# Three quarters of an expert's first product by Strassen's seven products, with operands reloaded from DRAM and sums kept in SBUF

## The chip, the core and the metric

The kernel runs on one core of one Trainium2 chip. The core has TensorE for matrix products (it writes to PSUM), VectorE (DVE in the profile), ScalarE (ACT), GpSimd (POOL) and SyncE (SP), which issues the transfers here. The metric is the device time of one launch in microseconds (us), the median of the timed runs.

## The reference

Attention without a softmax, and two experts one after the other, on 4608 tokens (8 batches of 576) with 512 features:

```python
kv = einsum('bhsd,bhse->bhde', k, v)           # per batch and head, 64 x 64
out = einsum('bhsd,bhde->bhse', q, kv)
x = out / sqrt(mean(out * out) + 1e-6) * g_norm    # then [4608, 512]

h = x @ w_in                                   # first expert: 512 -> 2048
x = (h * cos(h)) @ w_out                       # 2048 -> 512

h = x @ w_in2                                  # second expert: 512 -> 1024
s = h * softmax(h)
x = (s - mean(s)) / sqrt(var(s) + 1e-6) * g_ln @ w_out2   # 1024 -> 512
```

All inputs and the output are 32-bit floats (the weights come as 64-bit words and are converted on the chip).

## The kernel before

Each large product is made three times, for accuracy: every operand is split into a high part (a rounded copy, written by ScalarE) and a low part (the rest, a subtraction on VectorE or GpSimd), and the helper `mm3` adds high x high, high x low and low x high into one PSUM bank. Its three lines are L175, L176 and L177. A matmul takes 128 x 128 weights and up to 512 columns.

**First expert.** The hidden units are cut into four quarters, one pass over all tokens for each. A pass has 9 blocks of 512 tokens and 4 chunks of 128 hidden units, so 36 steps. `step_h` makes the chunk's hidden values: 4 x 3 matmuls into one of two banks, then ScalarE and VectorE in turn (scale to an integer, L590; difference, L592; sine, L595; product, L598; high part, L600; low part, L601). `step_out` adds the chunk's part of the output to four banks (`acc0` to `acc3`), 4 x 3 matmuls, one step later. After four chunks `evac` takes the four banks: in pass 1 it copies them, in passes 2 to 4 it adds the sum so far, loaded from DRAM (`px2`, L618), on VectorE (L628), and stores it again (L633). So each of the four passes has 36 x 24 matmuls. x stays in SBUF for all passes and is split again for each (`prep_x`: ScalarE L562, GpSimd L567). The weights of the next pass are converted and split during a pass (`convert`, four VectorE operations L502 to L509; `split_w`).

**Pass 1** also holds the attention, in small matmuls between the steps (L372, L431, and transposes L462).

**Second expert.** Two token tiles of 128 form a pair, 18 pairs. The first product is already made by Strassen's scheme: the pair's rows and the features are cut into halves, four sums on GpSimd (L660) give the operands (`prep_pair`), and seven products of 2 x 3 matmuls replace eight (`second`). Seven sums on VectorE (L698) put the result together; each product starts a new one of four banks. Then follow the softmax and the norm (`soft`), 16 transposes (L771) and two times 24 matmuls (`second_out`).

**Order.** Everything is handed to a planner (`Flow`), which orders the work of each engine once, before the launch, from a duration and a due time per task. Each engine runs its queue in that order and waits on semaphores. SyncE's queue, which issues the transfers, is one of them. The planner never runs a task of GpSimd beside one of VectorE that has no operand in PSUM (`port`).

## Time and profile before

| | |
|---|---|
| median of 3 timed runs | 1299.99 us (1299.46 to 1300.11) |
| span of the profiled execution | 1297.6 us (2.4 us below that median) |
| busy: TensorE, VectorE, ScalarE, GpSimd | 98%, 68%, 53%, 35% |
| TensorE's granted clock, whole span | 0.996 |
| transfers | 139.58 MB, 108 GB/s |

The span runs from the first to the last instruction of the profiled execution, 1297.6 us; its own time has no other reading here, and the timed runs are other executions. Busy is the time in which an engine had an instruction in work. PEld is the loading of weights, which runs beside TensorE's matmuls. A row of a view names the line, the engine, the operation, and what it writes `<-` what it reads.

### The profile page before, as it was taken

Reading aid. Unit: us, or ns where it says so; the run is one execution under the profiler, and the core shown is the slowest. Engines: PE = TensorE matmul, PEld = TensorE weight load, DVE = VectorE, ACT = ScalarE, POOL = GpSimd, SP = SyncE. Lnnn points to the kernel's source line nnn. Section 1 sums busy time; section 2 is a strip of 40 time slices with the busy share of each in tenths; the row PEclk is TensorE's granted clock in tenths of the full one; section 3 lists DMA queues with packets and bytes.
Section 4 is the critical chain, followed back from the end, with each engine's and each line's share of the span. In section 5 each row is a group of like instructions: output and inputs, shape, how many; then the busy total and the mean of one; then the engine's idle time right before and its main releaser. Section 6 shows DMA issues by size and latency. Waiting matters only on the chain.

```text
span 1297.6 us, 17765 instructions
## 1 busy us (share of the span) xinstructions
PE 1276.8 (98%) x6468; PEld 1056.6 (81%) x6468; DVE 884.1 (68%) x1421; ACT 681.3 (53%) x1211; POOL 460.3 (35%) x437
## 2 busy tenths in 40 slices
PE   5999999999999999999999999999999999999998
PEld 4788888888888888888888888887888888888886
DVE  6885444688965457645454868788978787777854
ACT  4676455666554445454545555546454445444532
POOL 2336354557551337231313465432242222221100
PEclk8999999999999999999999999999999999999999
DMA  9654442243543244323233444544110111010000
GB/s 320 219 175 134 142 142 88 77 136 119 176 127 117 78 127 133 109 86 108 88 100 112 142 134 143 187 150 138 52 63 17 65 50 62 21 57 25 25 25 33
DMA packets 62407, 139.58 MB, mean 108 GB/s; under 512 B 7408, under 2 KB 10480, under 8 KB 61168
## 3 DMA queue, kind: packets, MB, share of 16 engines
q1 hardware_dynamic: 62320, 138.45, 33.2%
q8 instruction: 51, 0.84, 0.3%
q14 instruction: 36, 0.29, 0.1%
HBM read 91.23 MB, written 47.19 MB: 107 GB/s over the span
## 4 chain that ended last, share of the span: by engine, by line
PE 95%; DMA 1%; DVE 1%; ACT 1%; POOL 1%; issue 0%; SPq 0%; DVEq 0%; ACTq 0%
PE ps_acc L175 15%; PE ps_acc L177 15%; PE ps_acc L176 15%; PE ps_h L175 14%; PE ps_h L177 14%; PE ps_h L176 14%; PE ps_o L431 2%; PE ps_acc L771 2%; PE ps_o L372 1%; PE ps_o L462 1%; DMA att<-qkv 1%; DMA xt<-qkv 1%; POOL att L446 1%; DVE xt L738 0%; ACT xt L468 0%
## 5 line engine op out<-in xcount | busy, mean ns | idle before, releaser
L567 POOL TENSOR_TENSOR xhl<-xt,xhl 128x512 fp32r<-128x512 f32 (+3 forms) x176 | 191.9, 1120 | 227.6 <-ACT xhl L562 227.5
L175 PE MATMUL ps_acc<-temps,wpool 128*128 128x512 f32 x648 | 255.1, 394 | 0.0
L177 PE MATMUL ps_acc<-temps,wpool 128*128 128x512 f32 x648 | 252.5, 390 | 0.0
L176 PE MATMUL ps_acc<-temps,wpool 128*128 128x512 f32 x648 | 252.3, 389 | 0.0
L175 PE MATMUL ps_h<-xhl,wpool 128*128 128x512 f32 x576 | 228.0, 396 | 0.2 <-DVE temps L598 0.2
L177 PE MATMUL ps_h<-xhl,wpool 128*128 128x512 f32 x576 | 224.7, 390 | 0.0
L176 PE MATMUL ps_h<-xhl,wpool 128*128 128x512 f32 x576 | 224.6, 390 | 0.0
L592 DVE SCALAR_TENSOR_TENSOR temps<-ps_h,temps 128x512 f32<-128x512 f32 x144 | 99.2, 689 | 132.4 <-ACT temps L590 132.3
L601 DVE TENSOR_TENSOR temps<-temps,temps 128x512 fp32r<-128x512 f32 x144 | 124.5, 865 | 66.6 <-ACT temps L600 64.5
L590 ACT ACTIVATE temps<-ps_h 128x512 int32<-128x512 f32 x144 | 86.1, 598 | 142.2 <-PE ps_h L177 141.2
L595 ACT ACTIVATE temps<-temps,const 128x512 f32<-128x512 f32 x144 | 104.2, 724 | 89.7 <-DVE temps L592 89.5
L177 PEld LDWEIGHTS ps_acc<-temps,wpool 128*128 128x128 f32 x648 | 121.6, 188 | 25.9 <-DVE wpool L525 0.5
L175 PEld LDWEIGHTS ps_acc<-temps,wpool 128*128 128x128 f32 x648 | 121.7, 188 | 25.2 <-issue 0.3
L176 PEld LDWEIGHTS ps_acc<-temps,wpool 128*128 128x128 f32 x648 | 121.8, 188 | 24.2
L598 DVE TENSOR_TENSOR temps<-ps_h,temps 128x512 f32<-128x512 f32 x144 | 98.9, 687 | 59.6 <-ACT temps L595 59.4
L600 ACT CAST temps<-temps 128x512 fp32r<-128x512 f32 x144 | 89.4, 621 | 90.2 <-DVE temps L598 84.8
L175 PEld LDWEIGHTS ps_h<-xhl,wpool 128*128 128x128 f32 x576 | 108.4, 188 | 23.1 <-DVE temps L598 0.6
L177 PEld LDWEIGHTS ps_h<-xhl,wpool 128*128 128x128 f32 x576 | 108.4, 188 | 22.9
L176 PEld LDWEIGHTS ps_h<-xhl,wpool 128*128 128x128 f32 x576 | 108.5, 188 | 21.5
L562 ACT CAST xhl<-xt 128x512 fp32r<-128x512 f32 (+3 forms) x192 | 90.3, 510 | 10.0 <-PE ps_h L177 8.9
L754 POOL TENSOR_TENSOR xt<-xt,const 128x1 f32<-128x1 f32 x36 | 23.0, 639 | 196.1 <-DVE xt L751 188.6
L777 DVE TENSOR_TENSOR wpool<-ps_acc,wpool 128x512 fp32r<-128x512 f32 x72 | 46.6, 685 | 42.7 <-ACT wpool L774 42.7
(130 smaller groups left out, 2236.4 us busy)
## 6 DMA issues: line engine op xcount, KB each, us to landing
px<-temps SPq DMA_DIRECT2D x144, 256.0 KB, 2.7
temps<-px SPq DMA_DIRECT2D x108, 256.0 KB, 3.8
xt<-w SPq DMA_DIRECT2D x27, 512.0 KB, 4.6
att<-qkv SPq DMA_DIRECT2D x24, 512.0 KB, 5.1
rawp<-w SPq DMA_DIRECT2D x21, 512.0 KB, 3.9
xt<-px SPq DMA_DIRECT2D x9, 1024.0 KB, 5.3
out<-temps SPq DMA_DIRECT2D x36, 256.0 KB, 2.0
att<-qkv SPq DMA_DIRECT2D x24, 288.0 KB, 5.6
```

Of the source, the lines that this page charges most:

```text
L175: PE.matmul(ps, lhsT=lh, rhs=rh, start=start, stop=False)
L176: PE.matmul(ps, lhsT=lh, rhs=rl, start=False, stop=False)
L177: PE.matmul(ps, lhsT=ll, rhs=rh, start=False, stop=stop)
L562: ACT.copy(out=buf["xh", i][:, k, a - m * TB:a - m * TB + n], in_=xt(k, a, n))
L567: eng.tensor_tensor(out=buf["xl", i][:, k, r], in0=xt(k, a, n), in1=f(buf["xh", i][:, k, r]), op=ALU.subtract)
L590: add("ACT", 0.61, lambda: ACT.activation(out=buf["kk"], in_=h(), func=AF.Copy, scale=INV_2PI, bias=0.25), r=[hb], w=["kk"], at=at)
L592: add("DVE", 0.71, lambda: DVE.scalar_tensor_tensor(out=buf[tk], in0=h(), scalar=INV_2PI, in1=buf["kk"], op0=ALU.mult, op1=ALU.subtract), ...
L595: add("ACT", 0.74, lambda: ACT.activation(out=buf[tk], in_=buf[tk], func=AF.Sin, bias=buf["halfpi"][:, 0:1], scale=2 * math.pi), r=[tk, "h ...
L598: add("DVE", 0.71, lambda: DVE.tensor_tensor(out=buf[tk], in0=h(), in1=buf[tk], op=ALU.mult), r=[hb, tk], w=[tk], at=at, ps=True)
L600: add("ACT", 0.64, lambda: ACT.copy(out=buf[ghk], in_=buf[tk]), r=[tk], w=[ghk], at=at + 2)
L601: add("DVE", 0.71, lambda: DVE.tensor_tensor(out=buf[glk], in0=buf[tk], in1=f(buf[ghk]), op=ALU.subtract), r=[tk, ghk], w=[glk], at=at + 2)
L777: DVE.tensor_tensor(out=buf["ll", n][:, part, :], in0=tr(), in1=f(buf["lh", n][:, part, :]), op=ALU.subtract)
```

## The change

Pass 1 stays. The other three quarters of the first expert become 15 **items**: a block of token tiles by one quarter. The blocks hold 3, 3, 4, 4 and 4 pairs of tiles (`BLOCKS`), so a matmul has 384 columns in the first two and 512 in the others (one column per token of one half of the pairs). A quarter has two halves of 256 hidden units. `first_h` makes one half for the block by seven products; the tokens' two halves, the features' two halves and the hidden units' two halves are the 2 x 2 quarters of Strassen's scheme. Three of the products are added in PSUM to a bank that holds an earlier one (`more=True`), the other sums are VectorE's. `first_out` makes the output part as before and adds it to sums in SBUF (`acc`), which are loaded before a block's first quarter and stored after its last.

x no longer stays in SBUF: pass 1 writes it to DRAM (`xd`), and each block loads it, forms the sums on GpSimd, and splits them (`prep`, L624 and L391/L392), once for its three quarters. The weights of these quarters, and those of the second expert, are converted and split once, during pass 1 and the items, and written to DRAM (`wid`, `wod`, `bd`, `lwd`); each item loads its own into two buffers (`reload_in`, `reload_out`). The low parts of the items' activations are GpSimd's (L674). The second expert's products use the same scheme with adding in PSUM, so five sums on VectorE (L859).

```diff
-NPASS, CPP = 4, 4
+BLOCKS = (0, 3), (6, 3), (12, 4), (20, 4), (28, 4)
...
-    def evac(ps_, m, px, at):
...
-                add("DVE", 0.71, lambda d=d, sk=sk: DVE.tensor_tensor(out=buf[sk], in0=buf[ACC[d]][:, 0:TB], in1=buf[sk],
-                                                                      op=ALU.add), r=[ACC[d], sk], w=[sk], at=at, ps=True)
...
+    def reload_in(fp, at):
+        s = fp % 2
+        for n_, (pos, n) in enumerate(((B11, 2), (T1, 2), (T3, 2), (T4, 1))):
+            wide = slice(pos * 256, (pos + n) * 256)
+            add("SP", 0.8 * n, lambda wide=wide: SP.dma_start(out=f(rwi(s)[:, :, wide]), in_=wid[fp, :, :, wide]),
+                r=[("wid", fp, o) for o in range(pos, pos + n)], w=[("wi", s, o) for o in range(pos, pos + n)],
+                at=at + 2 * n_, lat=2.0)
...
+    def first_h(T, s, at, step):
...
+        def prod(bk, a, b, t, more=False):
+            for kk in range(2):
+                def mm(kk=kk):
+                    w = slice(b * 256 + kk * P, b * 256 + kk * P + P)
+                    x = rx(a)
+                    mm3(buf[bk][:, 0:n], rwi(s)[:, 0, w], rwi(s)[:, 1, w], x[:, 0, kk, 0:n], x[:, 1, kk, 0:n],
+                        kk == 0 and not more, kk == 1, more)
...
+        prod(bA, A11, B11, at)
...
+        prod(bB, S2, T2, at + d)
+        plus(v1, bB, v0, at + 2 * d + E_)
+        prod(bC, S1, T1, at + 2 * d)
+        plus(v2, bC, v1, at + 3 * d + E_)
+        prod(bA, A12, B21, at + 3 * d, more=True)
+        chain(bA, True, 0, 0, at + 4 * d)
+        prod(bB, S3, T3, at + 4 * d)
+        plus(v2, bB, v2, at + 5 * d + E_)
+        chain(v2, False, 1, 1, at + 5 * d)
+        prod(bC, S4, B22, at + 5 * d, more=True)
+        plus(bC, bC, v1, at + 6 * d + E_)
+        chain(bC, True, 1, 0, at + 6 * d)
+        prod(bB, A22, T4, at + 6 * d, more=True)
+        plus(bB, bB, v1, at + 7 * d + E_)
+        chain(bB, True, 0, 1, at + 7 * d)
...
+    def first_out(item, half, at, step):
...
+            if item["first"]:
+                add("SP", e_(0.8, 0.4, n), lambda ak=ak, place=place: SP.dma_start(out=parted(buf[ak][:, 0:n], T), in_=place()),
+                    r=pk, w=[ak], at=t - 16, lat=2.0)
+            for c in range(4):
...
+                    mm3(buf[bk][:, 0:n], w[:, 0, :], w[:, 1, :], rg(m)[:, 0, 0:n], rg(m)[:, 1, 0:n], c == 0, c == 3)
...
+            add("DVE", e_(0.71, 0.44, n), lambda ak=ak, bk=bk: DVE.tensor_tensor(
+                out=buf[ak][:, 0:n], in0=buf[bk][:, 0:n], in1=buf[ak][:, 0:n], op=ALU.add),
+                r=[bk, ak], w=[ak], at=t - 4, ps=True)
```

`rx` are the split operands of x (single, written anew for each block), `rwi` and `rwo` the two buffers for weights, `rg` twelve places for activations. A `chain` is the cosine with its two parts.

Three places of the order. First TensorE in the middle of the first expert. Before, where in pass 4 a chunk's hidden values end and an output part begins (`ps_acc` are the output's banks, `ps_h` those of the hidden values):

```order
L177 MATMUL ps_h_142<-xhl_91,wpool_70 128x512
L175 MATMUL ps_h_142<-xhl_91,wpool_70 128x512
L176 MATMUL ps_h_142<-xhl_91,wpool_70 128x512
L177 MATMUL ps_h_142<-xhl_91,wpool_70 128x512
L175 MATMUL ps_h_142<-xhl_91,wpool_70 128x512
L176 MATMUL ps_h_142<-xhl_91,wpool_70 128x512
L177 MATMUL ps_h_142<-xhl_91,wpool_70 128x512
L175 MATMUL ps_acc_129<-temps_96,wpool_70 128x512 [waits Activation_49]
L176 MATMUL ps_acc_129<-temps_96,wpool_70 128x512 [waits DVE_49]
L177 MATMUL ps_acc_129<-temps_96,wpool_70 128x512
L175 MATMUL ps_acc_130<-temps_96,wpool_70 128x512
L176 MATMUL ps_acc_130<-temps_96,wpool_70 128x512
```

After the change, in the first item, the last product of one half and one of the other half (`ps_167` and `ps_163` are banks, `rxb`, `rxa` the operands of x, `rwi_794` and `rwi_795` the two buffers for weights):

```order
L171 MATMUL ps_0_167<-rxb_2474,rwi_794 128x384 [waits DVE_49]
L172 MATMUL ps_0_167<-rxb_2474,rwi_794 128x384
L173 MATMUL ps_0_167<-rxb_2474,rwi_794 128x384
L171 MATMUL ps_0_167<-rxb_2474,rwi_794 128x384
L172 MATMUL ps_0_167<-rxb_2474,rwi_794 128x384
L173 MATMUL ps_0_167<-rxb_2474,rwi_794 128x384
L171 MATMUL ps_0_163<-rxa_81,rwi_795 128x384
L172 MATMUL ps_0_163<-rxa_81,rwi_795 128x384
L173 MATMUL ps_0_163<-rxa_81,rwi_795 128x384
L171 MATMUL ps_0_163<-rxa_81,rwi_795 128x384
L172 MATMUL ps_0_163<-rxa_81,rwi_795 128x384
L173 MATMUL ps_0_163<-rxa_81,rwi_795 128x384
```

Where four times three matmuls of 512 columns stood for a chunk, each product has two times three, here of 384 columns; the first waits for VectorE.

Second TensorE in the last products of a pair of the second expert. Before, three products in three banks (`late_r` and `wpool` hold the weights' parts, `xhl_91` the pair's):

```order
L175 MATMUL ps_h_1_6711<-wpool_69,xhl_91 128x512
L176 MATMUL ps_h_1_6711<-wpool_69,xhl_91 128x512
L177 MATMUL ps_h_1_6711<-wpool_69,xhl_91 128x512
L175 MATMUL ps_h_0_2167<-late_r_4276,xhl_91 128x512 [waits DVE_49]
L176 MATMUL ps_h_0_2167<-late_r_4277,xhl_91 128x512
L177 MATMUL ps_h_0_2167<-late_r_4276,xhl_91 128x512
L175 MATMUL ps_h_0_2167<-wpool_69,xhl_91 128x512
L176 MATMUL ps_h_0_2167<-wpool_69,xhl_91 128x512
L177 MATMUL ps_h_0_2167<-wpool_69,xhl_91 128x512
L175 MATMUL ps_h_1_2168<-late_r_4278,xhl_91 128x512 [waits DVE_49]
L176 MATMUL ps_h_1_2168<-late_r_4279,xhl_91 128x512
L177 MATMUL ps_h_1_2168<-late_r_4278,xhl_91 128x512
```

After, the end of the product S3 T3, the product S4 B22, and the start of A22 T4:

```order
L171 MATMUL ps_0_187<-rxa_81,rwi_795 128x512
L172 MATMUL ps_0_187<-rxa_81,rwi_795 128x512
L173 MATMUL ps_0_187<-rxa_81,rwi_795 128x512
L171 MATMUL ps_0_191<-rxa_81,rwi_795 128x512 [waits DVE_49]
L172 MATMUL ps_0_191<-rxa_81,rwi_795 128x512
L173 MATMUL ps_0_191<-rxa_81,rwi_795 128x512
L171 MATMUL ps_0_191<-rxa_81,rwi_795 128x512
L172 MATMUL ps_0_191<-rxa_81,rwi_795 128x512
L173 MATMUL ps_0_191<-rxa_81,rwi_795 128x512
L171 MATMUL ps_0_187<-rxb_2474,rwi_795 128x512 [waits DVE_49]
L172 MATMUL ps_0_187<-rxb_2474,rwi_795 128x512
L173 MATMUL ps_0_187<-rxb_2474,rwi_795 128x512
```

The product A22 T4 now goes to the bank of S3 T3, `ps_187`, with one product between; the wait for VectorE at its start is for the sum that reads this bank.

Third VectorE. Before, where pass 2 ends and pass 3 begins (`temps` are the cosine's and the running sum's buffers, `rawp` a weight chunk in conversion):

```order
L592 SCALAR_TENSOR_TENSOR temps_95<-ps_h_142,temps_95 128x512 [waits Activation_49]
L628 TENSOR_TENSOR temps_97<-ps_acc_129,temps_97 128x512 [waits DMAHW6_49,PE_49]
L628 TENSOR_TENSOR temps_98<-ps_acc_130,temps_98 128x512 [waits DMAHW7_49,PE_49]
L598 TENSOR_TENSOR temps_95<-ps_h_142,temps_95 128x512 [waits Activation_49]
L628 TENSOR_TENSOR temps_99<-ps_acc_131,temps_99 128x512 [waits DMAHW0_49,PE_49]
L628 TENSOR_TENSOR temps_100<-ps_acc_132,temps_100 128x512 [waits DMAHW3_49,PE_49]
L601 TENSOR_TENSOR temps_96<-temps_95,temps_96 128x512 [waits Activation_49]
L502 TENSOR_SCALAR rawp_2174<-rawp_2174 128x512 [waits Activation_49]
L592 SCALAR_TENSOR_TENSOR temps_95<-ps_h_141,temps_95 128x512 [waits Activation_49]
L504 SCALAR_TENSOR_TENSOR rawp_2174<-rawp_2172,rawp_2174 128x512 [waits DMAHW4_49,DVE_49]
L509 SCALAR_TENSOR_TENSOR rawp_2177<-rawp_2173,rawp_2177 128x512
L598 TENSOR_TENSOR temps_95<-ps_h_141,temps_95 128x512 [waits Activation_49]
```

After, at the first item of tokens 2560 to 3583 (`mid` and `fh` hold the output sums, `rxa` and `rxb` the new operands of x, `fconv` a weight chunk in conversion):

```order
L805 TENSOR_TENSOR mid_2483<-ps_0_183,mid_2483 128x512 [waits PE_49]
L805 TENSOR_TENSOR fh_115<-ps_0_171,fh_115 128x512 [waits PE_49]
L392 TENSOR_TENSOR rxb_2474<-xf_110,rxb_2474 128x4x128 [waits DMAHW5_49,Activation_49]
L392 TENSOR_TENSOR rxb_2474<-xf_110,rxb_2474 128x2x128 [waits Activation_49]
L365 TENSOR_SCALAR fconv_101<-fconv_101 128x512
L805 TENSOR_TENSOR fh_115<-ps_0_175,fh_115 128x512 [waits PE_49]
L367 SCALAR_TENSOR_TENSOR fconv_101<-fconv_101 128x512 [waits DMAHW2_49,DVE_49]
L392 TENSOR_TENSOR rxb_2474<-xf_111,rxb_2474 128x4x128 [waits DMAHW7_49,Activation_49]
L392 TENSOR_TENSOR rxa_80<-sf_105,rxa_80 128x4x128 [waits Activation_49]
L392 TENSOR_TENSOR rxb_2474<-xf_111,rxb_2474 128x2x128 [waits Activation_49]
L805 TENSOR_TENSOR mid_2478<-ps_0_179,mid_2478 128x512 [waits PE_49]
L370 TENSOR_SCALAR fconv_101<-fconv_101 128x512 [waits DVE_49]
```

Between the output sums (L805) now stand the splits of the block's x (L392) and the conversions (L365, L367), in one queue.

## Rows read from the trace of the kernel before

**Rows 1.** Head of the page: span; busy us, share, instructions of each engine.

```profile
span 1297.6 us, 17765 instructions
...
PE 1276.8 (98%) x6468; PEld 1056.6 (81%) x6468; DVE 884.1 (68%) x1421; ACT 681.3 (53%) x1211; POOL 460.3 (35%) x437
```

**Rows 2.** The page's chain that ended last, by engine and by line.

```profile
PE 95%; DMA 1%; DVE 1%; ACT 1%; POOL 1%; issue 0%; SPq 0%; DVEq 0%; ACTq 0%
PE ps_acc L175 15%; PE ps_acc L177 15%; PE ps_acc L176 15%; PE ps_h L175 14%; PE ps_h L177 14%; PE ps_h L176 14%; PE ps_o L431 2%; PE ps_acc L771 2%; PE ps_o L372 1%; PE ps_o L462 1%; DMA att<-qkv 1%; DMA xt<-qkv 1%; POOL att L446 1%; DVE xt L738 0%; ACT xt L468 0%
```

**Rows 3.** Stages by time: length, busy us of each engine, granted clock, DMA.

```profile
core 0: us, PE busy (x) PEld busy (x) DVE busy (x) ACT busy (x) POOL busy (x), PEclk, DMA share, GB/s
30.00:294.00 264.00, 262.86 (x1780) 217.33 (x1777) 166.04 (x254) 166.24 (x311) 123.21 (x114) 1.00 0.44 141
294.00:886.00 592.00, 591.83 (x2611) 489.58 (x2610) 387.13 (x569) 306.52 (x538) 243.92 (x210) 1.00 0.40 125
887.00:1297.60 410.60, 405.13 (x1917) 335.09 (x1915) 311.64 (x564) 195.24 (x342) 84.09 (x100) 1.00 0.12 45
```

**Rows 4.** Timeline of TensorE in pass 3: start, length drawn, line.

```profile
599.62 0.39 PE L175 MATMUL ps_h<-xhl,wpool 128*128 128x512 f32 x1
...
605.06 0.39 PE L175 MATMUL ps_h<-xhl,wpool 128*128 128x512 f32 x1
```

**Rows 5.** Weight loads by line and form: busy us, mean ns.

```profile
L175 PEld LDWEIGHTS ps_h<-xhl,wpool 128*128 128x128 f32 x576 | 108.4, 188 | 23.1 <-DVE temps L598 0.6 <-issue 0.3
```

**Rows 6.** Timeline of TensorE in the second expert: transposes, next matmul.

```profile
1011.41 1.04 PE L771 MATMUL ps_acc<-const,xt 128*128 128x128 f32 x8
1012.20 0.49 PE L175 MATMUL ps_h<-late_r,xhl 128*128 128x512 f32 x1
```

**Rows 7.** Views of single lines: ns min/median/max, first and last start.

```profile
L601 DVE TENSOR_TENSOR temps<-temps,temps x144: 674/692/1795, 43.5 to 886.5; 128x512 fp32r<-128x512 f32 x144
...
L598 DVE TENSOR_TENSOR temps<-ps_h,temps x144: 673/691/693, 40.6 to 885.0; 128x512 f32<-128x512 f32 x144
...
L678 DVE TENSOR_TENSOR xhl<-xt,xhl x72: 409/681/1220, 860.2 to 1228.7; 128x512 fp32r<-128x512 f32 x54, 128x256 fp32r<-128x256 f32 x18
...
L502 DVE TENSOR_SCALAR rawp<-rawp x21: 413/419/1511, 251.8 to 520.0; 128x512 uint32<-128x512 uint32 x21
...
L504 DVE SCALAR_TENSOR_TENSOR rawp<-rawp,rawp x21: 675/686/1791, 254.2 to 525.8; 128x512 uint32<-128x512 uint32 x21
...
L676 ACT CAST xhl<-xt x72: 389/623/651, 859.4 to 1224.9; 128x512 fp32r<-128x512 f32 x54, 128x256 fp32r<-128x256 f32 x18
...
L567 POOL TENSOR_TENSOR xhl<-xt,xhl x176: 450/1280/1812, 108.5 to 840.0; 128x512 fp32r<-128x512 f32 x88, 128x256 fp32r<-128x256 f32 x32, 128x384 fp32r<-128x384 f32 x28, 128x128 fp32r<-128x128 f32 x28
...
L525 POOL TENSOR_TENSOR wpool<-rawp,wpool x21: 1285/1299/1752, 259.2 to 535.9; 128x512 fp32r<-128x512 f32 x21
...
L660 POOL TENSOR_TENSOR xt<-xt x36: 726/736/1747, 846.3 to 1207.1; 128x256 f32<-128x256 f32 x36
```

**Rows 8.** The cosines' first VectorE operation in pass 1 (0 to 294 us).

```profile
L592 DVE SCALAR_TENSOR_TENSOR temps<-ps_h,temps x36: 676/691/694, 37.3 to 293.8; 128x512 f32<-128x512 f32 x36
```

**Rows 9.** L601 in the page's costliest groups: busy us, mean ns.

```profile
L601 DVE TENSOR_TENSOR temps<-temps,temps 128x512 fp32r<-128x512 f32 x144 | 124.5, 865 | 66.6 <-ACT temps L600 64.5
```

**Rows 10.** The first 100 us by time (columns as in rows 3).

```profile
0.00:25.00 25.00, 12.79 (x124) 11.06 (x124) 13.82 (x28) 8.88 (x16) 8.61 (x14) 0.93 0.96 325
25.00:100.00 75.00, 72.24 (x585) 59.74 (x585) 63.77 (x112) 51.70 (x98) 27.08 (x28) 0.95 0.61 200
```

**Rows 11.** DMA issues of the page: count, KB each, us to landing.

```profile
temps<-px SPq DMA_DIRECT2D x108, 256.0 KB, 3.8
```

**Rows 12.** Timeline of TensorE at the start of the second expert.

```profile
907.68 0.50 PE L177 MATMUL ps_acc<-wpool,wpool 128*128 128x512 f32 x1 [0.91 <-DVE wpool L777]
```

**Rows 13.** Timeline: last matmul of a product, then its sum.

```profile
1016.43 0.39 PE L177 MATMUL ps_h<-late_r,xhl 128*128 128x512 f32 x1
...
1016.85 0.68 DVE L698 TENSOR_TENSOR xt<-ps_h,temps 128x512 f32<-128x512 f32 x1
```

More of the change, by code (lines that the diff above doesn't have):

```diff
@@ new lines, in open_e2, with parted, rwi, rwo @@
+    def open_e2():
+        close_pool("rg2")
+        open_pool("e2a", side="right")
+    BANKS = [("bank", i) for i in range(8)]
+    for i in range(8):
+        declare(f"ps{i}", ("bank", i), 0, [P, 512])
+        open_pool(f"ps{i}", space=PSUM)
+    def parted(ap, l=2):
+        return ap.rearrange("p (l n) -> p l n", l=l)
+    def rwi(s):
+        return parted(buf["rwi", s])
+    def rwo(s):
+        return buf["rwo", s].rearrange("p (d j l n) -> p d j l n", d=KC, j=2, l=2)
+    def rg(m):
+        return parted(buf["rg", m])
@@ new lines, in tile_kernel, with att_bank @@
+    stage = Ring(("st", i) for i in range(7))
+    hvs = Ring(("hv", i) for i in range(4))
+    tts = Ring(("tt", i) for i in range(3))
+    xfs = Ring(("xf", i) for i in range(2))
+    xns = Ring(("xn", i) for i in range(2))
+    sfs = Ring(("sf", i) for i in range(2))
+    wss = Ring(range(2))
+    early = [*BANKS[2:8]]
+    late_att = Ring(BANKS[6:8])
+    accs = Ring(BANKS[2:6])
+    hbank = Ring([BANKS[0], BANKS[1], BANKS[6], BANKS[7]])
+    def att_bank():
+        return early.pop(0) if early else late_att()
@@ L408, in parts @@
         return res
+    held = {}
     def tile_slots(g):
-        bks = [next_bank() for _ in range(2)]
+        bks = [att_bank() for _ in range(2)]
         def heads(ap):
@@ new lines, in tile_kernel, with end_step @@
+    n_jobs = len(jobs)
+    last = None
+    closed = False
+    def end_step(m, c, j, at):
+        step_out(c, j, at)
+        if c == CPP - 1:
+            block_out(m, at)
+    for i in range(NSTEP):
+        m, c = divmod(i, CPP)
+        at, d = t_step(i), STEP_A
+        if c == 0 and m + 1 < NB:
+            run_slots(needs[m + 1] - pos, at + SLOT_LATE, SLOT_RATE, needs[m + 1])
+        if pos == len(slots) and not closed and m == NB - 2:
+            closed = True
+            flow.change(open_p1, ("att",), ("rx0", "rx1", "rx6", "mid", "rg2x"))
+            flow.change(lambda: None, ("p0s",), ("p1h",))
+            for g in range(NU - 2, NU):
+                pair_prep(g, at)
+            stage.keys, stage.n = [("st", i) for i in range(4, 7)], 0
+        while jobs and (n_jobs - len(jobs)) * (JOB1 - JOB0) <= (i - JOB0) * n_jobs:
+            jobs.pop(0)(at + JOB_AT)
+        step_h(m, c, i % 2, at)
@@ L914, in tile_kernel @@
         if last:
             end_step(*last)
-        if ps_ and c == 1:
-            px = load_px(m, at - 4)
-        last = (ps_, m, c, i % 2, px, at + 2.5 * d)
-        block = ps_ * NB + m + 1
-        if c == 1 and block < NPASS * NB:
-            prep_x(block, at + 2)
-            if ps_ == NPASS - 1:
-                for part in range(NX):
-                    if m * TB < (part + 1) * XP - TB <= (m + 1) * TB:
-                        flow.change(lambda: None, (f"xt{part}",), (f"late_x{part}",))
@@ L926, in tile_kernel @@
-        if ps_ == NPASS - 1 and m == NB - 1 and c == CPP - 2:
-            load_block(0, at)
-    assert not queue
-    prep_pair(0, at - 4)
-    flow.change(lambda: None, ("xo1",), ("xs1",))
-    flow.change(open_second, ("ps_h",), ("ps_h21",))
-    end_step(*last)
-    for old, new in (("steps", "snaps"), ("gs", "late_g"), ("w1", "late_w1")):
-        flow.change(lambda: None, (old,), (new,))
+        last = (m, c, i % 2, at + 2.5 * d)
+    assert not jobs and closed
+    end_step(*last)
+    T1_ = t_step(NSTEP)
@@ L935, in tile_kernel @@
+    assert not jobs
+    flow.change(lambda: None, ("p1t", "tts"), ("e2t",))
+    stage.keys = [("su", i) for i in range(6)]
+    flow.change(lambda: None, ("conv",), ("e2c",))
+    for i in range(2):
+        flow.change(lambda: None, (f"wo{i}",), (f"lhl{i}",))
+    for c in range(NC):
+        flow.change(lambda: None, (f"rg{c}",), (f"lw{c}",))
+        add("SP", 1.6, lambda c=c: SP.dma_start(out=f(rg(c)), in_=lwd[c]), r=[("lwd", c)], w=[("lw", c)],
+            at=T_E2 + c, lat=2.0)
     for u in range(NU):
-        at = t_step(NPASS * NSTEP) + PAIR_C * u
```

946 lines of the change are left out of this document (531 added, 415 removed).

## Prediction

> **What bounds the kernel now.** I read the head of the profile first: TensorE is busy 98% of 1297.6 us, the next engine, VectorE, 68% [rows 1]. A busy TensorE can hide waits, since a matmul is drawn 0.39 us long while the next one starts 0.23 us after it, so I went on to the chain of waits and to the stages. The chain is 95% TensorE, nearly all of it the three lines of one helper on the two kinds of PSUM bank [rows 2]. Then the stages: pass 1 with the attention (30 to 294 us), passes 2 to 4 (294 to 886), the second expert (887 to the end). In the middle one TensorE is idle for 0.2 us of 592, and the granted clock is 1.00, the upper of its two levels, 2.4 GHz [rows 3]. Last the timeline: between 599.62 and 605.06 us 24 matmuls start, one every 0.2267 us [rows 4]. So passes 2 to 4 are a queue of 3 x 36 x 24 = 2592 matmuls without a gap: 2592 x 0.2267 = 587.5 of the stage's 592 us. Each matmul removed there is worth 0.227 us, as long as nobody else becomes late.
>
> **The change, part by part.** *Matmuls removed.* Pass 1, the attention and the second expert keep theirs. Passes 2 to 4 become 15 items: a block of token tiles by a quarter of the hidden units. Each item has two halves of 7 products x 2 x 3 = 42 matmuls, where 48 stood for the same work, and 96 output matmuls as before: 180 for 192, at 512 columns in nine items (1620) and at 384 columns in six (1080).
>
> The price at 512 columns is 0.2267 us. No row has this matmul at 384. From below: all of it shrinks with the columns, 0.170. From above: the weight load's own busy time, 0.188 [rows 5], if the next matmul had to wait for the whole of it. Between: 128 columns less at 2.4 GHz are 0.0533 us, which leaves 0.1733. I take this one: eight transposes, each with a 128x128 weight load, pass from 1011.41 to 1012.20 us, 0.10 us each [rows 6]. So one load can follow another far sooner than 0.17 us, and its drawn time is no floor. The Trainium skill gives a smaller load in "TensorE: Matmul & The Clock Gate", section LDWEIGHTS (loading the stationary operand): its columns divided by 1.2 GHz, an estimate of 0.107 us at 128. By that rule the price stays 0.1733 and the saving 33.1 us, by the drawn 0.188 it would be 17.3 us; the transposes side with the rule.
>
> Passes 2 to 4 then need 1620 x 0.2267 + 1080 x 0.1733 = 367.2 + 187.2 = 554.4 us, **33.1 us less** than 587.5 (36.7 less at 0.170, 17.3 less at 0.188).
>
> *VectorE.* In pass 1 it now splits x as well (GpSimd did most of it) and converts 23 weight chunks for later. Between the first and the last cosine of pass 1 its queue holds 70 cosine operations, 34 low parts, 43 splits, 64 operations of the attention and 5 sums, 216 at about 0.69 us, and 23 conversions of two operations at 0.42 and two at 0.69 [rows 7]: 149 + 51 = 200 us. These cosines start 37.3 to 293.8 us from the beginning, 256 us apart [rows 8]; today VectorE is busy 166 of 264 us there [rows 3]. So it fits in TensorE's time, and I cost pass 1 at nothing. The cover is 56 us of slack; beyond it each us on VectorE would be one of the kernel.
>
> An item has 10 sums of a product with a kept one, 8 output sums and 16 cosine operations, 34 x 0.69 = 23.5 us of VectorE against 40.8 of TensorE (less of both at 384 columns). A block's first item has the splits on top, and some items conversions for the second expert. The fullest is the first of tokens 2560 to 3583: its stretch of the queue (cosine to cosine) holds 56 operations at 0.69 (16 cosine, 12 + 11 sums, 14 splits, 3 scaled) and three conversions' 12: 38.6 + 6.7 = 45.3 us, against 180 x 0.2267 = 40.8. I let the excess reach TensorE, **4.5 us**. It may also sink into the next items, which have room (0), or grow: the mean of L601 is 0.865 [rows 9], 0.17 over its median, and 31 all-SBUF operations drawn out so much are 5.4 us more (10).
>
> *GpSimd* gets the low parts of the items' activations, eight per item at 1.3 us [rows 7], and the differences of the weights. Here it stands in VectorE's way: the all-SBUF L601 takes 0.692 us in the median and up to 1.795, GpSimd's L567 up to 1.812, while L598 with an operand in PSUM never passes 0.693 [rows 7]. So one waits until the other's operation ends, and the all-SBUF work of both must fit into an item end to end. By the same medians it is 20 to 30 us in most items, and 15 + 24 = 39 us in the fullest (the first of tokens 1536 to 2559, 40.8 us long). It fits, so nothing is added, but a wait of this kind can stand in front of a sum that TensorE needs (second rival).
>
> *Transfers.* The operands go to DRAM once and come back for each block: 3.67 MB for the first and 2.1 MB for the second product per item, 5.8 MB in 31.2 us (185 GB/s) or in 40.8 us (141 GB/s). Today's trace moves 325 GB/s in its first 25 us, and 200 GB/s at a busy share of 0.61 [rows 10]. A half's operands are free after its own products and needed 23 us later; those of the second product come free column group by column group and are needed some 15 us later. A 256 KB load lands in 3.8 us [rows 11]. So they lie beside the matmuls. The running sum goes to DRAM and back with 40 loads and 76 stores for 108 and 144; it was hidden, so this gains nothing.
>
> *Block changes.* New x operands can be written only after the last product with the old ones; the order puts 108 output matmuls, 24.5 us, between. A block's 16 splits are 16 x 0.69 on VectorE and 16 x 0.62 on ScalarE, its 16 sums on GpSimd 16 x 0.74 [rows 7]: each fits alone, in a row they don't. Four such changes and the one into the second expert (7.3 MB to load, 22 us at 325 GB/s) may show 0 to 4 us each. Nearest is today's start of the second expert, with one idle of 0.91 us [rows 12]. I take about half of it at four places, **2 us**.
>
> *Second expert.* A pair's sums on VectorE fall from seven to five, but its last product adds into the bank that VectorE has just read. One product lies between, so TensorE gets there 7 x 0.2267 = 1.59 us after the start of the last matmul before the sum. VectorE starts 0.42 us after such a start (1016.43 to 1016.85) and takes 0.68 [rows 13], 1.10 us. That leaves over 0.4 us: nothing is added, if VectorE stands ready.
>
> Sum: 1297.6 - 33.1 + 4.5 + 2.0 = 1271.0 us of span. The profiled execution's span lies 2.4 us below the median of the timed runs (1299.99); with it 1273.4, **1273 us**.
>
> **The rivals.** *The weight load is a floor at 384 columns* (0.188 us): it saves 17.3 for 33.1, 1289 us. For it the drawn time, against it the transposes. 4%.
>
> *VectorE is late for the sum between two products that share a bank; slower than before.* Each item has two such places and each pair of the second expert one, 30 + 18 = 48. With 0.4 us of slack, an all-SBUF operation held to L601's longest (1.795) in front of each sum costs 1.4 us there, 67 us in all. From 0.55 us at each place on (26.4 us) the gain left is gone; at 0.9 us it is 1273 + 43 = 1316 us. The Trainium skill has the mechanism in "SBUF — State Buffer", section Who interferes with whom: GpSimd and a VectorE operation with two SBUF inputs exclude each other for a whole instruction. By that rule the case is open wherever such an operation precedes the sum. For it: queues are in order, and one late conversion delays all behind it. Against it: in the second expert two splits stand there, with 2.7 us for them, and in the items output matmuls lie between many of these products. 8%.
>
> *Reloads and block changes take it back*: 15 items at 0.5 to 1.5 us, since SyncE issues in order and one transfer that waits for a sum holds those behind: 1281 to 1296, most likely 1287 us. For it: nearly twice the bytes. Against it: the slack above. 16%.
>
> *Less is lost than I allow* (the excess sinks in, and some of today's short stalls vanish): 1264 to 1268 us, 14%, counted with the forecast.
>
> **How the numbers follow.** The forecast, 1264 to 1281 us, has 72%, the weight load 4%, the reloads 16%, the late sums 8%. The likeliest time is 1273. The range of 1264 to 1289 takes in the prices at 384 columns (1270 to 1289), the bounds of the excess and most of the reload case; it leaves out that one's upper end and the slower case. A measurement of this kernel tells a change from none at about 0.2%, 2.6 us. Faster: 72 + 4 + 13 = 89%. The same: 3%, the reloads' upper end. Slower: 8%.
>
> **What would show it.** Right: the helper's matmuls 0.227 us apart at 512 and 0.173 at 384 columns; 555 to 562 us for the items; a pass 1 that ends within 5 us of today's; idle time of TensorE at the first item of tokens 2560 on. Wrong: 0.188 us at 384 columns; idle time on the helper's lines in every item, ended by a DMA (reloads) or by VectorE's sums at the end of each half (late sums); a pass 1 longer by more than 5 us, which would be VectorE's new work.

## The result

The changed kernel takes 1288.05 us (median of 4 runs, 1286.71 to 1289.03) against 1299.72 us of the kernel before on the same chip: a ratio of 0.9912, 95% interval 0.9898 to 0.9926. It is faster by 11.7 us; the forecast was 26.7 us. The direction is right and the time lies in the range, but the gain is less than half of the forecast.

The head of the profile of the changed kernel answers to [rows 1]:

```profile
span 1284.8 us, 18847 instructions
...
PE 1254.4 (98%) x6576; PEld 1063.7 (83%) x6576; DVE 924.8 (72%) x1544; ACT 679.3 (53%) x1225; POOL 515.2 (40%) x510
```

TensorE is still busy 98%. That number hides what happened: the stages by time, with the columns of [rows 3], say more. Pass 1 ends at 302.0 us (300.4 before), the 15 items at 875.9, and from there to the end it is 408.9 us.

```profile
core 0: us, PE busy (x) PEld busy (x) DVE busy (x) ACT busy (x) POOL busy (x), PEclk, DMA share, GB/s
30.00:302.00 272.00, 268.04 (x1813) 222.27 (x1810) 206.30 (x326) 181.66 (x336) 150.06 (x141) 0.99 0.83 272
302.00:876.00 574.00, 566.71 (x2702) 494.36 (x2701) 420.02 (x671) 285.12 (x514) 281.69 (x256) 1.00 0.78 252
421.90:426.10 4.20, 4.20 (x16) 4.20 (x16) 2.79 (x5) 3.05 (x7) 4.20 (x5) 0.59 1.09 368
876.00:1284.80 408.80, 403.80 (x1909) 333.34 (x1907) 280.79 (x515) 199.73 (x353) 74.58 (x100) 1.00 0.15 51
```

I give the items by their matmuls, since every one of the helper's has its row: from the start of the 865th (the first behind pass 1's 864) to that of the second expert's first, 574.0 us pass, where the same stretch took 588.3 before (300.4 to 888.7). So the items saved 14.3 us, pass 1 gave back 1.6, and the second expert neither gained nor lost 0.1. The third row above, 4.2 us, is a stretch that I come to below.

The 2700 matmuls of the items (1632 at 512 columns and 1068 at 384, as the cut falls) need 1632 x 0.2267 + 1068 x 0.1733 = 555.1 us at the forecast's prices. The other 18.9 us lie in the distances from one matmul's start to the next, added up from their rows:

```
what the distances have over 0.2267 (512 columns) or 0.1733 us (384)
33 distances with more than 20 ns over it (stalls)   11.4 us
   302 to 324 us, first block                         4.5 us
   418 to 426 us, second block                        4.7 us
   570 us                                             1.7 us
   the others                                         0.6 us
2667 distances with less (spacing)                    7.5 us
```

**Stalls.** The waits of TensorE in three stretches (what it waited for, us in total, times, longest):

```profile
PE ps L171 <- DVE fh L671: 1.2, 1, 1.2
PE ps L172 <- DVE rxa L392: 1.2, 2, 0.9
...
PE ps L172 <- DMA rwi<-wid: 2.8, 1, 2.8
...
PE ps L172 <- POOL rg L674: 1.4, 1, 1.4
```

In the first block the rows name VectorE for 2.4 of the 4.5 us: a split of x (L392) and a cosine's product (L671); 0.6 more is ScalarE's (L766). The second is a reload of weights, the third a low part on GpSimd. Behind the second the clock falls: the row 421.90 to 426.10 above has a granted clock of 0.59, and the timeline there has matmuls 0.32 us apart at 384 columns, which is the lower of the two levels, 1.2 GHz:

```profile
421.68 0.44 PE L172 MATMUL ps<-rg,rwo 128*128 128x384 f32 x1 [2.83 <-DMA rwi<-wid]
...
424.01 0.52 PE L172 MATMUL ps<-rg,rwo 128*128 128x384 f32 x1
424.33 0.52 PE L173 MATMUL ps<-rg,rwo 128*128 128x384 f32 x1
...
426.32 0.34 PE L171 MATMUL ps<-rxb,rwi 128*128 128x384 f32 x1
426.49 0.34 PE L172 MATMUL ps<-rxb,rwi 128*128 128x384 f32 x1
```

From the start before it (418.51) to that of the first row 3.2 us pass, 3.0 more than usual, and a little later ten matmuls take 0.147 us more each. With the smaller excess of three others this stall cost 4.7 us, not 3.0.

**Spacing.** This I had not looked for. Twelve matmuls of one kind, in the middle of the items, where nothing waits:

```profile
665.99 0.40 PE L171 MATMUL ps<-rxb,rwi 128*128 128x512 f32 x1
666.23 0.39 PE L172 MATMUL ps<-rxb,rwi 128*128 128x512 f32 x1
...
668.56 0.39 PE L173 MATMUL ps<-rxb,rwi 128*128 128x512 f32 x1
668.79 0.39 PE L171 MATMUL ps<-rg,rwo 128*128 128x512 f32 x1
```

From 665.99 to 668.79 us twelve matmuls start, one every 0.2333 us, where [rows 4] have 0.2267. At 384 columns the price is as forecast: 105 output matmuls start from 476.17 to 494.32 us, 0.1745 apart, though their weight loads are drawn 0.19 us long:

```profile
476.17 0.34 PE L171 MATMUL ps<-rg,rwo 128*128 128x384 f32 x1
...
479.99 0.19 PEld L173 LDWEIGHTS ps<-rg,rwo 128*128 128x128 f32 x1
480.16 0.19 PEld L171 LDWEIGHTS ps<-rg,rwo 128*128 128x128 f32 x1
...
494.32 0.34 PE L173 MATMUL ps<-rg,rwo 128*128 128x384 f32 x1
```

### The profile page after: what moved, and what is told of

The parts are those of the page before. It is cut to its first block, busy times and chain, and to the rows that moved or that the text cites. A ratio compares the mean times of both kernels' runs of the same rounds, so it can differ in the third digit from the quotient of the medians.

```text
span 1284.8 us, 18847 instructions
## 1 busy us (share of the span) xinstructions
PE 1254.4 (98%) x6576; PEld 1063.7 (83%) x6576; DVE 924.8 (72%) x1544; ACT 679.3 (53%) x1225; POOL 515.2 (40%) x510
## 4 chain that ended last, share of the span: by engine, by line
PE 92%; DMA 3%; DVE 2%; ACT 1%; POOL 1%; issue 1%; SPq 0%; POOLq 0%; DVEq 0%
PE ps L171 28%; PE ps L172 28%; PE ps L173 28%; PE ps L549 2%; PE ps L929 2%; PE ps L492 1%; PE ps L586 1%; DMA rwi<-wid 1%; DMA xf<-xd 1%; DMA att<-qkv 1%; DMA bd<-ws 1%; DMA pa<-w 0%; POOL rg L674 0%; ACT xf L590 0%; POOL att L567 0%
## 5 line engine op out<-in xcount | busy, mean ns | idle before, releaser
L172 PE MATMUL ps<-rg,rwo 128*128 128x512 f32 (+1 forms) x912 | 347.5, 381 | 4.3 <-DMA rwi<-wid 2.8
L171 PE MATMUL ps<-rg,rwo 128*128 128x512 f32 (+1 forms) x912 | 349.8, 384 | 0.0
L173 PE MATMUL ps<-rg,rwo 128*128 128x512 f32 (+1 forms) x912 | 346.9, 380 | 0.0
L674 POOL TENSOR_TENSOR rg<-fh,rg 128x512 fp32r<-128x512 f32 (+1 forms) x120 | 148.6, 1249 | 171.7 <-ACT rg L673 167.6
L172 PEld LDWEIGHTS ps<-rg,rwo 128*128 128x128 f32 x912 | 171.9, 188 | 34.6 <-POOL rg L674 5.8
L171 PEld LDWEIGHTS ps<-rg,rwo 128*128 128x128 f32 x912 | 171.8, 188 | 29.4 <-ACT fh L705 0.4
L173 PEld LDWEIGHTS ps<-rg,rwo 128*128 128x128 f32 x912 | 171.7, 188 | 29.4
L171 PE MATMUL ps<-rxa,rwi 128*128 128x512 f32 (+1 forms) x384 | 146.5, 382 | 0.8 <-DVE fh L859 0.8
L172 PE MATMUL ps<-rxa,rwi 128*128 128x512 f32 (+1 forms) x384 | 145.4, 379 | 1.2 <-DVE rxa L392 1.2
L173 PE MATMUL ps<-rxa,rwi 128*128 128x512 f32 (+1 forms) x384 | 145.2, 378 | 0.0
L669 ACT ACTIVATE fh<-fh,const 128x512 f32<-128x512 f32 (+1 forms) x156 | 106.4, 690 | 34.5 <-DVE fh L666 33.2
L171 PE MATMUL ps<-rxb,rwi 128*128 128x512 f32 (+1 forms) x288 | 112.1, 389 | 1.8 <-DVE fh L671 1.2
L673 ACT CAST rg<-fh 128x512 fp32r<-128x512 f32 (+1 forms) x156 | 90.5, 586 | 43.4 <-DVE fh L671 41.0
L172 PE MATMUL ps<-rxb,rwi 128*128 128x512 f32 (+1 forms) x288 | 110.1, 382 | 0.0
L173 PE MATMUL ps<-rxb,rwi 128*128 128x512 f32 (+1 forms) x288 | 110.1, 382 | 0.0
L666 DVE SCALAR_TENSOR_TENSOR fh<-ps,fh 128x512 f32<-128x512 f32 (+1 forms) x126 | 81.3, 649 | 36.3 <-ACT fh L664 33.9
L671 DVE TENSOR_TENSOR fh<-ps,fh 128x512 f32<-128x512 f32 (+1 forms) x126 | 81.1, 647 | 22.7 <-ACT fh L669 22.2
L805 DVE TENSOR_TENSOR mid<-ps,mid 128x512 f32<-128x512 f32 (+1 forms) x90 | 57.0, 634 | 47.5 <-PE ps L173 47.1
L624 POOL TENSOR_TENSOR sf<-xf 128x256 f32<-128x256 f32 x72 | 61.3, 858 | 60.1 <-DMA xf<-xd 40.1
L172 PEld LDWEIGHTS ps<-rxa,rwi 128*128 128x128 f32 x384 | 72.3, 188 | 13.5 <-DVE rxa L392 1.8
```

Of the source, the lines that this page charges most:

```text
L171: PE.matmul(ps, lhsT=lh, rhs=rh, start=start, stop=False, skip_group_check=more)
L172: PE.matmul(ps, lhsT=lh, rhs=rl, start=False, stop=False, skip_group_check=more)
L173: PE.matmul(ps, lhsT=ll, rhs=rh, start=False, stop=stop, skip_group_check=more)
L624: add("POOL", 0.75, lambda: POOL.tensor_tensor(out=out_(), in0=in0(), in1=in1(), op=fn), r=[*keys, *r], w=w, at=at)
L666: add("DVE", e_(0.71, 0.44, n), lambda: DVE.scalar_tensor_tensor(out=tt(), in0=h(), scalar=INV_2PI, in1=tt().bitcast(I32), op0=ALU.mult, o ...
L669: add("ACT", e_(0.74, 0.5, n), lambda: ACT.activation(out=tt(), in_=tt(), func=AF.Sin, bias=buf["halfpi"][:, 0:1], scale=TWO_PI), r=[tk, " ...
```

## The experiments

All ratios stand beside the kernel before on the same chip. e8, e9, e11 and e12 build on e5; in kernels with a pad, line numbers are up to 2 higher than in the changed kernel.

**What sets the spacing: e1 to e3, then e5.** The slow matmuls have something in common: their moving operand is `rxb` or `rg2`, two buffers on the right side of SBUF, and the build places this side at addresses that leave 32 modulo 64; the left side leaves 0. I moved sides by a small unused buffer, which leaves the order of the instructions on every engine as it is:

e1 (e3 has it too):

```diff
+    declare("padr", "padr", 0, [P, 8])
...
+    open_pool("padr", side="right")
     open_pool("att", side="right")
```

> All buffers of the right side of SBUF move by 32 bytes, so that every operand of the helper's matmuls starts at a multiple of 64 bytes. Theory (the start address of the moving operand sets the spacing): 984 matmuls at 512 columns fall from 233.5 to about 227 ns, 432 at 384 columns from 176.5 to 174, together 6.4 + 1.0 = 7.4 us less, 1288.05 to about 1280.6 us; the long stalls stay. Rival (the engine is slowed there by transfers or by the other engines' traffic, or by the high addresses as such): spacing and time stay, 1288 us.

e2:

```diff
+    declare("rwi", "padw", 0, [P, 8])
     for s in range(2):
         declare("rwi", ("rwi", s), 0, [P, 2 * NOP * 256], F32R)
```

> Only the two buffers of weights for the first product (the stationary operand of 2016 matmuls) move by 32 bytes, off the multiple of 64; moving operands stay where they are. Theory (only the moving operand counts): 1288 us, spacing of the matmuls with these weights unchanged. Rival (either operand counts): 864 matmuls at 512 and 288 at 384 columns that were at 227 and 174 ns rise by 6.6 and 2.3 ns, 6.4 us more, about 1294 us.

e3, beside the lines of e1:

```diff
+    declare("const", "padl", 0, [P, 8])
```

> The right side is aligned as in e1, and everything of the left side moves off the multiple of 64 bytes by 32. Theory (start address of the moving operand): now 3120 matmuls at 512 and 648 at 384 columns are slow, 984 and 432 fast: 2136 x 6.6 ns + 216 x 2.3 ns = 14.6 us more than the changed kernel, about 1303 us. Rival (high addresses or traffic): no change, 1288 us.

Measured: e1 1285.38 us (1281.88 to 1286.65; ratio 0.9886, 0.9872 to 0.9899), e2 1292.52 (0.9950, 0.9936 to 0.9963), e3 1288.94 (0.9926, 0.9903 to 0.9949). My theory, the moving operand's own alignment, fell twice: in e1 the `rxb` matmuls only went from 233.7 to 232.1 ns, though aligned, and in e3 nearly all moving operands were off the 64 and the kernel was not 15 us slower. e2's median came near the 1294 us of its rival, but in part by the clock: its runs go from 1287.11 us at a mean granted clock of 0.996, the profiled one, to 1294.60 at 0.992. That the stationary operand counts too is read from its rows. I then gave each matmul of the traces the addresses that it has in the built program and sorted the distances by the difference between its moving operand and the stationary operand of the matmul behind it (the one that is loaded meanwhile):

```
mean distance at 512 columns, 100 to 1290 us, ns (count), by that difference modulo 256 bytes
                 0             32           96           128          160
changed kernel   228.3 (2828)               233.5 (933)
e1               228.0 (2828)                            232.1 (935)
e2               228.3 (1976)  232.9 (852)  232.9 (357)  232.4 (576)
e3               228.8 (2828)                                         234.5 (933)
e5               227.1 (3762)
```

In all of them 0 is fast and every other difference slow at 512 columns, whichever side and whichever operand was moved; in e2 the matmuls with `rxa` and `rwi`, fast in the changed kernel (228.9 ns), are at 232.9. At 384 columns the difference of 32 is not seen where one such matmul follows another: 243 of them in e2 are 174.0 ns apart, as in the changed kernel. Which weights count, a matmul's own or those loaded meanwhile, the runs do not separate: the table sorts 42 matmuls of e2 with `rxa` under 0, since the weights behind them are `rwo`, but their own have the difference 32 and they take 233.7 ns (227.8 in the changed kernel). In e1 the difference was 128: it had not removed it. e5 does.

```diff
+    declare("padr", "padr", 0, [P, 40])
...
+    open_pool("padr", side="right")
```

> As e1, but the right side of SBUF moves by 160 bytes: every moving operand of the helper's matmuls and the stationary operand that is loaded beside it then have the same start address modulo 256. Theory (this difference sets the spacing; in e1 it was 128 for the 984 + 432 matmuls): they fall from 233.4 to 228.5 ns or below at 512 columns and from 176.5 to 174 at 384, 984 x 5 ns + 432 x 2.5 ns = 6 us less, and up to 11 us less if the excess of the other matmuls (228.4 for 226.7) comes from their neighbours; 1277 to 1282 us. Rival (the slow ones are slow by their place on the right side, whatever the offset): spacing stays above 232 ns, 1285 to 1288 us.

Measured 1278.97 us (1275.23 to 1283.66; ratio 0.9842, 0.9823 to 0.9861): 9.1 us faster than the changed kernel by 160 unused bytes. The same twelve matmuls in e5:

```profile
663.57 0.39 PE L171 MATMUL ps<-rxb,rwi 128*128 128x512 f32 x1
663.80 0.39 PE L172 MATMUL ps<-rxb,rwi 128*128 128x512 f32 x1
...
666.06 0.39 PE L173 MATMUL ps<-rxb,rwi 128*128 128x512 f32 x1
666.29 0.39 PE L171 MATMUL ps<-rg,rwo 128*128 128x512 f32 x1
```

663.57 to 666.29 us, 0.2267 apart. Over the items the spacing's excess falls from 7.5 to 0.4 us, in the second expert from 4.2 to 0.75, so most of what the matmuls without a difference had over 226.7 ns was their neighbours'. The rival (the place on the right side) fell. Other parts vary between executions of the same order: pass 1 ends at 302.0 us in the changed kernel, at 303.6, 301.3, 303.4 and 304.3 in e1, e2, e3 and e5. The kernel before has the same fault in its second expert, in the 414 matmuls whose moving operand lies on the right side (`late_r`):

e10, on the kernel before:

```diff
+    declare("padr", "padr", 0, [P, 56])
...
+    open_pool("padr", side="right")
```

> The kernel before, with its right side moved by 224 bytes so that all moving and stationary operands of the helper have the same start modulo 256. Theory of the offset: 414 matmuls of the second expert fall from 233 to 227 ns and their neighbours from 229 to 227, 2.5 to 4.4 us less: 1295.5 to 1297.5 us for 1299.8. Rival (the offset only counts with the changed kernel's traffic): 1300 us.

Measured 1296.40 us (ratio 0.9977, 0.9968 to 0.9986); `late_r` goes from 232.4 to 228.0 ns. So the offset costs without the change's traffic as well; the gain is as large as expected from the rows.

**Reloads: e4.**

```diff
-                reload_in(2 * q + i, h_at - 12 + i * h_dur / 2)
+                if n < 3: reload_in(2 * q + i, h_at - 12 + i * h_dur / 2)
...
+                    if n < 3: reload_out(2 * q + i, d, at + dur - 8 + 2 * d)
```

> The weights of the first expert are reloaded for the first block's three items only; the other twelve items use what is in the buffers (the numbers of these items' products are then not the reference's), 70 MB of loads less. Theory (the reloads are what TensorE waits for at 421.7 us): the 3.2 us stall there and the fall of the clock behind it (about 1.8 us) go, 1283 us; the stalls of the first item (302 to 324 us) stay. Rival (the transfers are hidden anyway, the wait named there is VectorE's or GpSimd's): 1288 us. A third: the load on the transfers also draws out the aligned matmuls (228.4 for 226.7 ns in the items), then another 1.5 to 3 us go, 1280 to 1282 us.

Measured 1283.71 us (ratio 0.9877, 0.9864 to 0.9891), 4.3 less. The stall at 421 us shrinks from 3.2 to 0.85 us from start to start, the clock stays up there, those at 532 and 570 us go, the first block's stay at 4.5. What is left at 420 us has another cause:

```profile
PE ps L172 <- POOL rg L674: 0.5, 1, 0.5
```

The items' stalls are 6.1 us, where the kernels with all reloads in the same order have 11.4 (changed), 12.0 (e1), 9.4 (e2), 8.0 (e3) and 10.5 (e5). So the load on the transfers does make stalls. That the reload itself is what TensorE waits for at 421 us holds for the one execution of the changed kernel: in e1, e2, e3 and e5 the same place waits 3.4, 1.3, 1.7 and 0.9 us for GpSimd's low part. In e1:

```profile
PE ps L172 <- POOL rg L676: 3.4, 1, 3.4
```

The spacing does not move (7.55 us), so the third theory fell: the load on the transfers is not what draws matmuls out.

**Conversions in pass 1: e6 and e9.**

e6 (the two numbers are `JOB0` and `JOB1`, the last of a longer line):

```diff
-SLOTS0, SLOT_T, SLOT_D, SLOT_LATE, SLOT_RATE, JOB0, JOB1 = 8, -12, 1, -16, 2.0, 5, 32
+SLOTS0, SLOT_T, SLOT_D, SLOT_LATE, SLOT_RATE, JOB0, JOB1 = 8, -12, 1, -16, 2.0, 4, 26
```

> The conversions for later quarters are spread over steps 4 to 26 of pass 1 in place of 5 to 32. Theory (at the first block's start VectorE is late because these conversions stand between its splits and its sums): the stalls of 302 to 324 us, 4.9 us, fall to 2 us or less, pass 1 ends within 2 us of before, 1285 us or less. Rival (the splits wait for x, that is for the transfers, or pass 1 has no room and grows by as much): no gain, 1288 us or more.

Measured 1288.98 us (ratio 0.9920, 0.9908 to 0.9932): no gain, as the rival had it. Pass 1 ends 1.2 us earlier, which is within what it varies by, but one stall of 5.5 us stands at 310 us and one of 2.8 at 325; the last split of the first block's x starts at 315.1 us, for 311.3 in the changed kernel. So the place of these conversions is not it alone.

e9:

```diff
-    jobs = [x for fp in range(2, NFP) for x in (job_in(fp), job_out(fp, 0), job_out(fp, 1))]
+    jobs = [x for fp in range(2, NFP - 2) for x in (job_in(fp), job_out(fp, 0), job_out(fp, 1))]
...
-SLOTS0, SLOT_T, SLOT_D, SLOT_LATE, SLOT_RATE, JOB0, JOB1 = 8, -12, 1, -16, 2.0, 5, 32
+SLOTS0, SLOT_T, SLOT_D, SLOT_LATE, SLOT_RATE, JOB0, JOB1 = 8, -12, 1, -16, 2.0, 5, 23
```

> e5 with the last six of pass 1's eighteen conversion jobs left out, at the same density, so that they end at step 23 of 36; the fourth quarter uses the third quarter's weights (its part of the result is not the reference's). Theory (in the first block's first item VectorE is late for its sums and splits because of these conversions): the stalls of 302 to 324 us fall from about 5 to under 2 us, and pass 1 ends 1 to 3 us earlier; about 1274 us against e5's 1279. Rival (the chain of x's load, sums, split and product is itself too long there): stalls stay at 4 to 5 us, 1278 us.

Measured 1268.70 us (ratio 0.9763, 0.9750 to 0.9777), 10.3 less than e5, more than the theory gave (the profiled executions differ by 8.8 us). The stalls of 302 to 325 us fall from 4.3 in e5 to 0.7 us (1.5 stand at 328 to 330), and all of the items' from 10.5 to 3.1: those at 421, 527 and 569 us go too, which the theory did not say. (That fewer spills and conversions then run on into these items is my reading; no run takes it apart. With the conversions their loads, splits and spills are gone too.) The stretch 302 to 324 us, the changed kernel first, then e9 (columns as in [rows 3]):

```profile
302.00:324.00 22.00, 19.05 (x98) 16.69 (x97) 16.73 (x28) 13.15 (x26) 15.59 (x15) 1.00 0.98 321
```

```profile
302.00:324.00 22.00, 21.61 (x119) 20.55 (x118) 13.11 (x25) 13.40 (x28) 12.06 (x12) 1.00 0.88 280
```

VectorE and GpSimd together are busy 32 of 22 us in the changed kernel, and 25 in e9. Without VectorE's operations that have a PSUM operand, 25 and 16 us are left, added up from their rows; these stand in each other's way [rows 7], so part of that is waiting drawn as busy. Laid over each other they cover 18.7 and 14.7 of the 22 us: the first has little room, but it is not full. What e9 changes is seen in the splits of the first block's x on VectorE (first and last start; the changed kernel, then e9):

```profile
L392 DVE TENSOR_TENSOR rxa<-sf,rxa x6: 678/948/1225, 278.3 to 311.3; 128x512 fp32r<-128x512 f32 x6
```

```profile
L394 DVE TENSOR_TENSOR rxa<-sf,rxa x6: 678/1050/1643, 275.4 to 291.4; 128x512 fp32r<-128x512 f32 x6
```

In the changed kernel the last of them starts 9 us into the first item, in e9 over 11 us before it. Pass 1 ends 1.3 us earlier than in e5 (303.0 for 304.3), which is within what it varies by.

**Blocks: e7.**

```diff
-BLOCKS = (0, 3), (6, 3), (12, 4), (20, 4), (28, 4)
+BLOCKS = (0, 4), (8, 4), (16, 4), (24, 3), (30, 3)
```

> The three blocks of four pairs come first, the two of three pairs last; so the block changes behind pass 1 have 40.8 us per item for the same reloads and conversions in place of 31. Theory (the stalls at 302 to 324 and at 421 us come from VectorE and the transfers, which the short items don't cover): most of 4.9 + 5.0 us goes, 1279 to 1283 us, unless the last block change and the second expert's operands then stall. Rival (the stalls come from the order in the queues): they move with the blocks, 1286 to 1290 us.

Measured 1298.11 us (ratio 0.9985, 0.9976 to 0.9993), 10 us slower than the changed kernel: both the theory and the rival had it wrong. My reading, which no run takes apart: a first block of four pairs has a third more splits, loads and sums to make while pass 1's conversions still run. The waits of 300 to 345 us are three long ones, and behind each stand matmuls of 512 columns 0.427 us apart, the lower clock again:

```profile
PE ps L171 <- ACT rxa L391: 5.5, 1, 5.5
PE ps L172 <- DVE rg L674: 3.7, 1, 3.7
PE ps L171 <- DVE fh L671: 3.4, 1, 3.4
```

**Low parts and order: e8, e11, e12.** At 570 us the chain of waits has this:

```profile
558.58 6.57 DMA bd<-ws
...
565.71 0.75 POOL ws L392
...
567.33 2.53 POOL rg L674 x2
...
569.90 0.50 PE ps L172
```

A store of the spill takes 6.6 us, the split into that spill buffer (L392, `ws`) waits for it in GpSimd's queue, and the low part that TensorE needs (L674) stands behind it. Three kernels try to get it out of there.

e8, in `chain`:

```diff
-                   [src], [("g", m)], [("gl", m)], t, False)
+                   [src], [("g", m)], [("gl", m)], t, True)
```

> e5 with the low parts of the items' activations on VectorE in place of GpSimd. Theory (the stalls at 421 and 569 us: the low parts stand in GpSimd's queue behind a split for the spill buffers, which waits for a slow store): these two places lose their 3.5 us of stalls; the other items stay; 1275 us against e5's 1279. Rival (VectorE is as full as these items: eight more operations of 0.69 us make it late): stalls on the helper's lines ended by VectorE in a block's first item, 4 to 10 us more, 1283 to 1289 us.

e11, in `spill`, `parts_out`, `reload_in` and `reload_out`; e12 also in `convert`, `prep_first`, `first_out` and `prep_second`:

```diff
-                at=at + 2 * n_, lat=2.0)
+                at=at + 2 * n_, lat=6.0)
```

> e5, and the planner counts 6 us in place of 2 from the issue of a spill or a reload to its landing (5 to 7 us in the trace), so that it puts other work of GpSimd ahead of a split whose spill buffer is not free yet. Theory (the stalls at 421 and 527 to 569 us come from low parts queued behind such a split): 4 of the 5.5 us of stalls behind 400 us go, 1275 us; the first block's 4 us stay. Rival (these stalls come from how much work there is, not from its order): 1278 to 1281 us.

> As e11, with 6 us also for the loads of weights to convert, of x for a block and of the running sums. Theory: as e11, and in the first block the conversions no longer stand ahead of sums while their words are still on the way: 2 us of its 4 go too, 1273 us. Rival: the amount of work decides there, as e9 says: no better than e11, within 2 us of it.

Measured: e8 1283.79 us (ratio 0.9882, 0.9867 to 0.9897), e11 1283.20 (0.9872, 0.9859 to 0.9886), e12 1289.61 (0.9924, 0.9911 to 0.9938); e5 has 1278.97. In e8 the stall at 569 us goes, as the theory has it, and the first block takes back more than that from VectorE, as the rival has it (4.8 us more appear at 475 to 501 us, around the start of the third block):

```profile
PE ps L171 <- DVE fh L673: 6.2, 2, 3.3
PE ps L172 <- DVE rxa L394: 1.4, 1, 1.4
PE ps L172 <- DVE rg L676: 1.2, 2, 0.9
```

In e11 the stalls at 421, 527 and 569 us go too (one of 1.5 us stays, at 540), so the mechanism is right for these three, and 8.6 us appear at 398 us, where the second block begins. A conversion (L365) waits in ScalarE's queue for its words, behind it stands the split of x (L393), then VectorE's part of it (L394) frees the buffer, and only then the next load of x can go. First the wait's row, then the chain ahead of it:

```profile
PE ps L171 <- ACT rxb L393: 8.3, 1, 8.3
```

```profile
383.23 6.37 DMA fconv<-w
389.63 0.68 ACT fconv L365
...
390.71 0.39 ACT rxb L393
...
393.13 0.98 DVE rxb L394
394.17 3.18 DMA xf<-xd
397.37 0.63 ACT rxb L393
```

e12 is worse still, by 6.4 us, which neither its theory nor its rival had. Each order that cleared one queue left another one waiting.

## Why the prediction was half right

- **Price at 384 columns** (0.1733): right, 0.1745. The rival of the weight load as a floor (0.188) is out: loads drawn 0.19 us long start every 0.173 us. The rule of the Trainium skill in "TensorE: Matmul & The Clock Gate", section LDWEIGHTS (loading the stationary operand), agrees with that, since an estimate of 0.107 us for a load leaves no floor there.
- **Price at 512 columns** (0.2267 for all 1620): the first step that failed. I took it from passes 2 to 4 [rows 4], where all operands have the same start modulo 256, and gave it to pairs of buffers that don't. It is 7.5 us of the items (5.8 at 512 columns, 1.7 at 384); e5 gives back 9.1 us, the second expert's share among them. The trace of before had the slow kind, in the second expert's `late_r`, and I had not compared it.
- **Block changes** (2 us) and **transfers** ("they lie beside the matmuls"): the second step that failed. The items' stalls are 11.4 us (8.0 to 12.0 with the same order in e1, e2, e3 and e5) against the 6.5 that I allowed, 4.5 for VectorE and 2 for the block changes. I counted 141 to 185 GB/s of reloads and left x, the running sums and the spills out; the items move 252 GB/s in the mean and 321 in their first 22 us. Without most reloads (e4) the kernel takes 4.3 us less: in the rows 3.9 us of stalls go at 418 to 426 us, clock included, and 2.1 at 532 and 570. The rival of reloads and block changes (16%) named 1287 us, nearest to what came, but by luck: it had a loss in every item, and what came is three places; and the stalls beyond the allowance are less than half of what was lost against the sum (4.9 of 13.8 us), the spacing more.
- **VectorE** (4.5 us in the first item of tokens 2560 to 3583): the size came out right by luck, the place was wrong. That item has no stall; the first block has, 4.5 us, with conversions of pass 1 (L365 to L372) running on into it and the splits of its x late. e9, with a third of pass 1's conversion jobs left out, takes most of that away. I had set GpSimd's work against VectorE's for the items, not for the end of pass 1, and the 56 us of slack of pass 1 is a sum over all of it, which says nothing of its end.
- **Pass 1** at nothing: 1.6 us in the profiled execution (0.8 to 3.9 with the same order in e1, e2, e3 and e5). **Second expert** at nothing: right, 408.9 us from 875.9 to the end, where before it was 408.8 (888.7 to 1297.6). The sums between products make almost nothing late: one wait of 0.8 us in the second expert (L859), none in the items (L754). The rival that ended slower than before is out.

With the measured terms the sum is 1297.6 - 33.1 + 7.5 + 11.4 + 1.6 = 1285.0, and the profiled execution's span is 1284.8.

What stays open: how much of the items' 8 to 12 us of stalls a better order could win. e9 shows that they hang on the amount of conversion, its loads and spills included; e6, e8, e11 and e12 moved them and made them longer (12.8 to 18.9 us). A third spill buffer was not tried. And why the offset modulo 256 matters is shown by no run, only that it does.
